# Phi fused into K's and Q's weights by six blocks of 120 rows instead of eight of 80

## Chip, cores and metric

The kernel runs on one core of a Trainium2 chip. The metric is the device time of one execution in microseconds (us), as a median over runs.

## What is computed

A token matrix x (2048 tokens of width D = 640) is normalised per row, and two branches and x itself are added. Branch A is a linear attention with 32 heads of width Dh = 20 (Hedgehog); branch B is a gated unit of width F = 1536. All tensors are bf16.

```
xn = layernorm(x)
q, k, v = split_heads(xn @ wqkv)                    # 32 heads of 20
pq, pk  = q @ w_phi[h], k @ w_phi[h]                # a 20 x 20 matrix for each head
phi_q = [softmax(pq), softmax(-pq)]; phi_k likewise # 40 features
kv = sum_s phi_k[s] * v[s];  z = sum_s phi_k[s]
A = (phi_q @ kv) / (phi_q @ z + 1e-6) @ wo
B = (silu(xn @ w1) * (xn @ w3)) @ w2
out = x + A + B
```

## The kernel before

Tokens are cut into 16 tiles of 128 (NST = 16), D into KD = 5 blocks of 128 and F into KF = 12. The order of the work is written out by hand, across all engines; every transfer is issued by SP, in program order, and each transfer takes the next of eight completion counters in turn.

1. **Start.** SP loads token tiles 0 and 1, V's weight and tiles 2 and 3. While they travel PE runs WARM = 19 products on a tile of zeros (L201), so that it is not idle. Tiles 0 to 3 are transposed by PE or DMA, normalised by DVE (L227, L269), and V of these four is made from the raw tiles (L298).
2. **Tiles 4 to 15.** They are loaded in pairs, normalised, and transposed by DMA into xnT (`by_dma`, L672). In between PE makes units of the gated branch (`glu_unit`, L442; the first, split, in L459) and V of each tile (`V`, L341 with the name pv).
3. **Fusion.** Since q @ w_phi is xn @ (wq @ w_phi), Phi goes into the weights once. `ldT` (L141) transposes columns of K's and Q's weight by DMA, NF = 8 pieces of FR = 80 rows (four heads each), into wkT and wqT. `phi_blocks` (L416, DVE) makes from w_phi and a 0/1 mask a block matrix for each piece, wphi, four heads of 20 columns wide. `fuse` (L426, PE) multiplies piece c of the transposed weight with block c, for each of the five 128-row blocks of the result, and two copies (L434, L435; ACT or DVE) bring its 640 columns from two banks to wkphi or wqphi, 320 columns each. K's fusion (`FB(0)` to `FB(4)`) stands at the end of stage 2, Q's in turns 4 to 8 of the next loop.
4. **K's loop**, 16 turns: `phi_unit` (products L341, name pk; exponentials L370; sums and reciprocals on DVE L404, L406; scaling on POOL L407), the product of phi_k and V (L483), and two units of the gated branch.
5. **Q's loop**, 20 turns: the same phi for Q (name pq), its DMA transpose, the product with kv (L518), the division, and `out_unit` (L581, L590), which sums the gated branch, wo and the residual and stores the tile.

The kernel takes exponentials without subtracting a maximum. A bound on the fused weights' norms decides whether that is safe; if it fails, the block below `tc.If(ok == 0)` (L880) computes the result anew with the maximum taken off. With this input the bound holds, and the block is jumped over. At the end (L926) SP waits for all eight completion counters, in their order, and the engines meet.

Of the kernel before, what the change touches and what calls it, by code (L numbers as in the profile page):

```python
# [8 lines left out]
P = 128  # L9
# [3 lines left out]
def kernel(  # L13
# [17 lines left out]
    nc = tc.nc  # L31
    bf = mybir.dt.bfloat16
# [5 lines left out]
    _, S, D = A_x.shape  # L38
    H, Dh = 32, 20
    F = B_w1.shape[1]  # L40
    NST, NSC, KD, KF = S // P, S // 512, D // P, F // P
    HD = D // 2
    EPS = 1e-5
    SAFE = 36.0
    BY_DMA = 4
    WARM = 19
    RAW = 4


# [2 lines left out]
    CH = 6 * 3 * Dh  # L52

    VC = 1 + 3 * Dh

    NF, FR = 8, 80

    x2 = A_x[0]
    out2 = out[0]
# [1 line left out]
    one = ctx.enter_context(tc.tile_pool(name="one", bufs=1))  # L61
# [8 lines left out]
    def pair(name):  # L70
        return psum2.tile([P, 2, 512], f32, name=name, tag="pair")
# [20 lines left out]
    wkT, wqT = [  # L92
        reg_w[:, i * NF * D : (i + 1) * NF * D].rearrange("p (c f) -> p c f", c=NF)
        for i in range(2)
    ]
# [13 lines left out]
    def slot(i):  # L109
        return phi[:, i].rearrange("p c g f -> p (c g f)")  # L110
# [3 lines left out]
    state = slot(3)[:, 0 : 2 * (NCH * VC - Dh)].bitcast(f32)  # L114
# [12 lines left out]
    def ld(dst, src):  # L127
        nc.sync.dma_start(out=dst, in_=src)  # L128
# [8 lines left out]
    wps = one.tile([P, NF, Dh], bf, name="wps")  # L137
    with tc.manual_schedule():
        def ldT(dst, i, c):
            a = i * D + c * FR  # L140
            nc.sync.dma_start_transpose(out=dst[:, c], in_=A_wqkv[:, a : a + P])  # L141


# [1 line left out]
        def ld_tiles(t, n):  # L145
            ld(
                xin[:, (t // 4) % 3, t % 4 : t % 4 + n],
                x2[t * P : (t + n) * P, :].rearrange("(t p) d -> p t d", p=P),
            )
# [7 lines left out]
        for c in range(KD):  # L157
# [9 lines left out]
        eps = one.tile([P, 1], f32, name="eps")  # L167
        nc.gpsimd.memset(eps[:], EPS)

        mask = one.tile([P, 4], bf, name="mask")  # L170
        nc.gpsimd.memset(mask[:], 1.0)
        nc.gpsimd.affine_select(
            out=mask[:], in_=mask[:], pattern=[[-20, 4]], base=0,
            channel_multiplier=1, compare_op=ALU.is_ge, fill=0.0,
        )
        nc.gpsimd.affine_select(
            out=mask[:], in_=mask[:], pattern=[[20, 4]], base=19,
            channel_multiplier=-1, compare_op=ALU.is_ge, fill=0.0,
        )

# [4 lines left out]
            out=own[:], in_=own[:], pattern=[[-64, 2], [-20, 3]], base=0,  # L185
# [3 lines left out]
            out=own[:], in_=own[:], pattern=[[64, 2], [20, 3]], base=19,  # L189
# [9 lines left out]
        def warm(n):  # L199
            for _ in range(n):  # L200
                nc.tensor.matmul(idle[:, 0:P], nought[:], nought[:])  # L201

        lit = nc.const_aps.tensor(1.0, [P, P], bf)
        for _ in range(2):
            nc.tensor.matmul(idle[:, 0:P], lit, lit)
        warm(WARM)

# [124 lines left out]
        def tile_of(t):  # L332
            return slice(t * P, (t + 1) * P)

        def by_token(cols, w, name, cut, ps=None):

            ps = ps or [bank(name), bank(name)]
            for c in range(KD):
                for i in range(2):
                    a, b = (0, cut) if i == 0 else (cut, D)  # L340
                    nc.tensor.matmul(  # L341
                        ps[i][:, 0 : b - a],
                        xnT[:, c, cols],
                        w[:, c, a:b],
                        start=(c == 0),
                        stop=(c == KD - 1),
                        skip_group_check=True,
                    )
            return ps

        def v_unit(dst, cols, ps=None):
            for piece in chunks(by_token(cols, wv, "pv", CH, ps)):
                v_copy(dst, *piece)
# [41 lines left out]
        def phi_unit(t, w, name, exps=exps, cols=None):  # L395

            ps = by_token(cols or tile_of(t), w, name, CH)
            dst = phi[:, t % 4]
            exps(ps, dst)
            rows = dst.rearrange("p c g f -> p (c g) f")[:, :, 0:60].rearrange(  # L400
                "p a (i d) -> p a i d", d=Dh
            )
            sk = work.tile([P, 2 * NCH, 3], f32, name="sk")
            nc.vector.reduce_sum(out=sk[:], in_=rows, axis=AX.X)  # L404
            rk = work.tile([P, 2 * NCH, 3], f32, name="rk")
            nc.vector.reciprocal(out=rk[:], in_=sk[:])  # L406
            nc.gpsimd.tensor_mul(  # L407
                out=rows, in0=rows, in1=rk[:, :, :, None].to_broadcast([P, 2 * NCH, 3, Dh])
            )

        wphi = one.tile([P, NF, 4, Dh], bf, name="wphi")

        def phi_blocks():
            nc.vector.tensor_mul(  # L416
                out=wphi[0:FR],
                in0=wps[0:FR, :, None, :].to_broadcast([FR, NF, 4, Dh]),
                in1=mask[0:FR, None, :, None].to_broadcast([FR, NF, 4, Dh]),
            )  # L420

        def fuse(dst, wT, d, ps, copy=None):

            for c in range(NF):
                b, i = divmod(c, 4)
                nc.tensor.matmul(  # L426
                    ps[b][:, FR * i : FR * (i + 1)],
                    wT[0:FR, c, d * P : (d + 1) * P],
                    wphi[0:FR, c],
                    start=(i == 0),  # L430
                    stop=(i == 3),
                    skip_group_check=True,
                )
            nc.scalar.copy(out=dst[:, d, 0:HD], in_=ps[0][:, 0:HD])  # L434
            (copy or nc.scalar.copy)(out=dst[:, d, HD:D], in_=ps[1][:, 0:HD])  # L435

        def glu_unit(sc, fi, banks=None):

# [40 lines left out]
        def kv_unit(t, v1, acc, first, last):  # L479

            for c in range(NCH):
                b, i = divmod(c, 6)
                nc.tensor.matmul(  # L483
                    acc[:, b, VC * i : VC * i + 1 + Dh * HC[c]],
                    phi[:, t % 4, c].rearrange("p g f -> p (g f)"),
                    v1[:, c, 0 : 1 + Dh * HC[c]],
                    start=(first and i == 0),
                    stop=last,
                    skip_group_check=True,
                )  # L490

        def kv_done(acc):

            for b, c0, n, k in ((0, 0, 6, 3), (1, 6, 4, 3), (1, 10, 1, 2)):
                a, e = VC * (c0 - 6 * b), 1 + Dh * k
                rows = acc[b][:, a : a + e * n].rearrange("p (c e) -> p c e", c=n)
                nc.vector.tensor_mul(
                    out=kvr[:, c0 : c0 + n, 0:k, 0:20],
                    in0=rows[:, :, 1:e].rearrange("p c (i d) -> p c i d", d=Dh),
                    in1=own[:, 0:1, 0:k, None].to_broadcast([P, n, k, Dh]),  # L500
                )
                nc.vector.tensor_mul(
                    out=kvr[:, c0 : c0 + n, 0:k, 20],
                    in0=rows[:, :, 0:1].to_broadcast([P, n, k]),
                    in1=own[:, 0:1, 0:k].to_broadcast([P, n, k]),
                )
# [150 lines left out]
        def unit(banks=None):  # L657
            return glu_unit(*glu.pop(0), banks)
# [12 lines left out]
        def by_dma(t):  # L671
            nc.sync.dma_start_transpose(out=xnT[:, :, tile_of(t)], in_=xin[:, (t // 4) % 3, t % 4, :])  # L672
# [78 lines left out]
        by_dma(6)  # L751
        by_dma(7)
        ld_tiles(14, 2)
        ld(wps[0:FR], A_w_phi.rearrange("h j f -> (h j) f").rearrange("(c p) f -> p c f", p=FR))
        g1()
        stats(8, 2)
        g3 = unit()
        g2()
        ldT(wkT, 1, 0)
        ldT(wkT, 1, 1)  # L760
        V(4)
        g3()
# [25 lines left out]
        V(11, two("pv"))  # L788
        ldT(wkT, 1, 4)
        ldT(wkT, 1, 5)  # L790
        ldT(wkT, 1, 6)
        g6 = unit()
        g6()
        lx(14, 2)
        by_dma(14)
        ldT(wkT, 1, 7)
        by_dma(15)
        V(12)
        g7 = unit()
# [12 lines left out]
        ps = by_token(tile_of(15), wv, "pv", CH)  # L812
# [66 lines left out]

    with tc.If(ok == 0):  # L880
        nc.gpsimd.memset(v_one[:, :, 0], 1.0)
        nc.gpsimd.memset(state, 0.0)
        halves = [state[:, 0 : 6 * VC], state[:, 6 * VC :]]
        with tc.For_i(0, NST, 1) as t:
            cols = bass.ds(t * P, P)
            v_unit(v_one, cols)
            phi_unit(0, wkphi, "pk", exps_less_max, cols)
            acc = pair("pkv")
            kv_unit(0, v_one, acc, True, True)
            for i, half in enumerate(halves):  # L890
                n = half.shape[1]
                nc.vector.tensor_tensor(out=half, in0=half, in1=acc[:, i, 0:n], op=ALU.add)
        kv_done(halves)
        with tc.For_i(0, NST, 1) as t:
            rows = bass.ds(t * P, P)
            phi_unit(0, wqphi, "pq", exps_less_max, rows)
            phi_transposed(0)
            r_unit(0, quotient_by_pool)
            o_transposed(0)
            h = hT[:, bass.ds(t, 1)].rearrange("p a f s -> p (a f) s")  # L900
            res = out_unit(h, slice(0, P), residual(rows))
            ld(out2[rows, :], res[:])
# [28 lines left out]
```

## Time and profile before

| | |
|---|---|
| time, median of 3 runs | 269.97 us (269.69 to 270.49) |
| profiled execution, time | 269.49 us |
| profiled execution, span of the trace | 267.8 us |
| granted TensorE clock, mean | 1.0 |
| busy: PE / DVE / ACT / POOL | 98% / 73% / 43% / 34% |
| DMA moved | 30.10 MB, mean 112 GB/s |

PE is TensorE's products, PEld its weight loads (which overlap the products), DVE is VectorE, ACT ScalarE, POOL GpSimd, and SPq the sequencer of SyncE, which issues transfers. L426 is line 426 of the kernel. In a chain or timeline the first number is the start in us after the span's start, the second the length in us; "idle before" tells how long the engine stood still ahead of an instruction, and what released it. Products are pipelined, so that the step from one to the next is shorter than the duration of one.

### The profile page before, as it was taken

To read this page: it belongs to the slowest core of one execution; us is meant where nothing else is said; L and a number is where in the kernel's file an instruction comes from. 1 tells how busy PE (TensorE), PEld (TensorE's weight loads), DVE (VectorE), ACT (ScalarE), POOL (GpSimd) and SP (SyncE) were. 2 spreads that over 40 slices of the span, in tenths; PEclk is the share of its full clock that TensorE was granted. 3 is DMA by queue.
4 is the path that set the end of the run, shared out by engine and by line. 5 is a ranking of instruction groups with operands and counts; after the bars stand their busy time and mean duration, and the time that the engine had idled before them with its cause. 6 is when DMAs were issued, how large, how long until landed. Compare 5 with 4: busy or idle time off the path is not lost.

```text
span 267.8 us, 5352 instructions
## 1 busy us (share of the span) xinstructions
PE 262.4 (98%) x2016; PEld 167.3 (62%) x2016; DVE 195.1 (73%) x363; ACT 114.7 (43%) x348; POOL 91.1 (34%) x88
## 2 busy tenths in 40 slices
PE   8999999999999999999999999999999999999993
PEld 7766565655555555555555555777777777777762
DVE  4789974397677777779997799967977776666431
ACT  5874454735566665445566655422222222220000
POOL 4052520064333333333544333344254333333000
PEclk9999999999999999999999999999999999999999
DMA  6999957999300000060000288856546574556631
GB/s 193 245 231 209 122 115 129 374 143 109 82 0 2 0 4 2 1 174 0 0 2 0 21 232 217 114 134 146 137 123 134 135 147 127 131 144 132 157 102 29
DMA packets 71967, 30.10 MB, mean 112 GB/s; under 512 B 58882, under 2 KB 70530, under 8 KB 71939
## 3 DMA queue, kind: packets, MB, share of 16 engines
q1 hardware_dynamic: 71938, 29.74, 50.7%
q8 instruction: 17, 0.28, 0.5%
q14 instruction: 12, 0.09, 0.2%
HBM read 13.14 MB, written 2.63 MB: 59 GB/s over the span
## 4 chain that ended last, share of the span: by engine, by line
PE 93%; DMA 3%; DVE 1%; SPq 1%; issue 0%; DVEq 0%
PE acc L581 28%; PE gp L442 19%; PE up L442 19%; PE pq L341 8%; PE pk L341 8%; PE pv L341 6%; PE pr L518 2%; PE pkv L483 2%; DMA xnT<-reg_h 1%; DMA reg_h<-in_A_x_dram 1%; SPq L128 1%; PE pf L426 1%; DVE st L227 1%; PE g L459 0%; PE gp L459 0%
## 5 line engine op out<-in xcount | busy, mean ns | idle before, releaser
L407 POOL TENSOR_TENSOR phi<-phi,rk 128x1320 bf16<-128x1320 bf16 x32 | 77.2, 2412 | 129.4 <-DVE rk L406 99.4
L442 PEld LDWEIGHTS <-w 128*128 128x128 bf16 x460 | 43.5, 98 | 47.9 <-DMA w<-in_B_w_dram 0.2
L404 DVE TENSOR_REDUCE sk<-phi 128x66 f32<-128x1320 bf16 x32 | 48.8, 1526 | 26.3 <-ACT phi L370 25.3
L442 PE MATMUL up<-xnT,w 128*128 128x512 bf16 x230 | 57.1, 379 | 0.0
L442 PE MATMUL gp<-xnT,w 128*128 128x512 bf16 x230 | 57.1, 379 | 0.0
L581 PE MATMUL acc<-reg_v,reg_h 128*128 128x320 bf16 (+2 forms) x384 | 54.9, 299 | 0.0
L341 PEld LDWEIGHTS <-xnT 128*128 128x128 bf16 x440 | 41.8, 98 | 19.1 <-DMA xnT<-reg_h 0.3
L370 ACT ACTIVATE phi<-pq 128x360 bf16<-128x360 f32 (+2 forms) x96 | 24.8, 366 | 57.7 <-issue 44.1
L581 PEld LDWEIGHTS <-reg_h 128*128 128x128 bf16 x384 | 37.3, 98 | 14.4
L453 ACT ACTIVATE th<-gp 128x512 f32<-128x512 f32 x47 | 28.4, 603 | 28.2 <-PE gp L442 28.2
L473 DVE SCALAR_TENSOR_TENSOR reg_h<-gs,up 128x512 bf16<-128x512 bf16 x47 | 32.3, 688 | 4.8
L470 DVE SCALAR_TENSOR_TENSOR gs<-th,gp 128x512 bf16<-128x512 f32 x47 | 30.9, 658 | 4.7 <-ACT th L453 4.7
L370 ACT ACTIVATE phi<-pk 128x360 bf16<-128x360 f32 (+2 forms) x96 | 24.9, 370 | 20.0 <-PE pk L341 20.0
L590 DVE TENSOR_TENSOR res<-acc,xr 128x320 bf16<-128x320 f32 (+2 forms) x32 | 14.2, 484 | 19.0 <-PE acc L581 19.0
L581 PE MATMUL acc<-reg_w,reg_v 128*128 128x320 bf16 (+2 forms) x160 | 24.5, 299 | 0.0
L341 PE MATMUL pk<-wkphi,xnT 128*128 128x360 bf16 (+1 forms) x160 | 24.4, 299 | 0.0
L341 PE MATMUL pq<-wqphi,xnT 128*128 128x360 bf16 (+1 forms) x160 | 24.3, 299 | 0.0
L406 DVE RECIPROCAL rk<-sk 128x66 f32<-128x66 f32 x32 | 18.1, 567 | 3.2
L581 PEld LDWEIGHTS <-reg_v 128*128 128x128 bf16 x160 | 15.7, 98 | 6.1
L341 PE MATMUL pv<-reg_w,xnT 128*128 128x360 bf16 x120 | 17.3, 299 | 0.0
L227 DVE BATCH_NORM_STATS2 st<-reg_h 128x6 f32<-128x320 bf16 x32 | 13.4, 476 | 4.3 <-DMA reg_h<-in_A_x_dram 4.3
L539 DVE TENSOR_TENSOR o__77<-pr,den 128x360 bf16<-128x360 f32 (+1 forms) x32 | 14.2, 485 | 0.6
(82 smaller groups left out, 161.3 us busy)
## 6 DMA issues: line engine op xcount, KB each, us to landing
w<-in_B_w_dram SPq DMA_DIRECT2D x2, 1280.0 KB, 8.2
xr<-in_A_x_dram SPq DMA_DIRECT2D x16, 160.0 KB, 2.5
out_dram<-res SPq DMA_DIRECT2D x15, 160.0 KB, 1.8
reg_h<-in_A_x_dram SPq DMA_DIRECT2D x6, 320.0 KB, 5.3
reg_v<-in_B_w_dram SPq DMA_DIRECT2D x1, 1920.0 KB, 8.5
w<-in_B_w_dram SPq DMA_DIRECT2D x4, 320.0 KB, 4.5
reg_w<-in_A_wqkv_dram SPq DMA_DIRECT2D x5, 160.0 KB, 3.3
reg_w<-in_A_wo_dram SPq DMA_DIRECT2D x1, 800.0 KB, 8.1
```

The lines of the kernel that those rows point to most:

```text
L227: nc.vector.bn_stats(out=st[:, i, :], in_=xt[:, i * HD : (i + 1) * HD])
L341: nc.tensor.matmul(ps[i][:, 0 : b - a], xnT[:, c, cols], w[:, c, a:b], start=(c == 0), stop=(c == KD - 1), skip_group_check=True,)
L370: nc.scalar.activation(out=dst[:, c0 : c0 + n, g, 0:k], in_=p.rearrange("p (c f) -> p c f", c=n), func=AF.Exp, scale=1.0 - 2.0 * g,)
L404: nc.vector.reduce_sum(out=sk[:], in_=rows, axis=AX.X)
L406: nc.vector.reciprocal(out=rk[:], in_=sk[:])
L407: nc.gpsimd.tensor_mul(out=rows, in0=rows, in1=rk[:, :, :, None].to_broadcast([P, 2 * NCH, 3, Dh]))
L442: nc.tensor.matmul(ps, w[:, c, fi * P : (fi + 1) * P], xnT[:, c, sc * 512 : (sc + 1) * 512], start=(c == 0), stop=(c == KD - 1),)
L453: nc.scalar.activation(out=th[:], in_=gp, func=AF.Tanh, scale=0.5)
L470: nc.vector.scalar_tensor_tensor(out=gs[:], in0=th[:], scalar=1.0, in1=gp, op0=ALU.add, op1=ALU.mult)
L473: nc.vector.scalar_tensor_tensor(out=hT[:, 4 * sc : 4 * sc + 4, fi, :], in0=gs[:].rearrange("p (t s) -> p t s", t=4), scalar=0.5, in1=up.r ...
L539: nc.vector.tensor_mul(out=o_[:, t % 2, Dh * h0 : Dh * h1].rearrange("p (h d) -> p h d", d=Dh), in0=p3[:, :, 0:20], in1=den[:, h0:h1, None ...
L581: nc.tensor.matmul(ps[:, 0 : b - a], rows[j][0], rows[j][1][:, a:b], start=(j == 0), stop=(j == len(rows) - 1),)
```

## The change

The weights' columns are cut into NF = 6 pieces of FR = 120 rows, six heads each. Since 640 is not a multiple of 120, the sixth piece starts at row 520 and overlaps the fifth; of its block only the last two heads (40 columns) are used. The first bank then holds three pieces (360 columns = CH), the second two pieces and the short one (280), and the copies are cut there. w_phi is loaded in two transfers: five pieces, then the overlapping one. Two `ldT` of K's weight are dropped, and two of Q's by the shorter loop. WARM becomes 20. In the block of the failed bound one memset of 651 columns becomes seven of 93.

```diff
-    WARM = 19
+    WARM = 20
...
-    NF, FR = 8, 80
+    NF, FR, LH = 6, 120, 6
+    AT = [120 * c for c in range(5)] + [D - 120]
...
-            a = i * D + c * FR
+            a = i * D + AT[c]
...
-        mask = one.tile([P, 4], bf, name="mask")
+        mask = one.tile([P, LH], bf, name="mask")
...
-        wphi = one.tile([P, NF, 4, Dh], bf, name="wphi")
+        wphi = one.tile([P, NF, LH, Dh], bf, name="wphi")
...
-                b, i = divmod(c, 4)
+                b, i = divmod(c, 3)
+                h0 = 4 if c == NF - 1 else 0
                 nc.tensor.matmul(
-                    ps[b][:, FR * i : FR * (i + 1)],
+                    ps[b][:, FR * i : FR * i + Dh * (LH - h0)],
                     wT[0:FR, c, d * P : (d + 1) * P],
-                    wphi[0:FR, c],
+                    wphi[0:FR, c, h0:LH],
                     start=(i == 0),
-                    stop=(i == 3),
+                    stop=(i == 2),
                     skip_group_check=True,
                 )
-            nc.scalar.copy(out=dst[:, d, 0:HD], in_=ps[0][:, 0:HD])
-            (copy or nc.scalar.copy)(out=dst[:, d, HD:D], in_=ps[1][:, 0:HD])
+            nc.scalar.copy(out=dst[:, d, 0:CH], in_=ps[0][:, 0:CH])
+            (copy or nc.scalar.copy)(out=dst[:, d, CH:D], in_=ps[1][:, 0 : D - CH])
...
-        ld(wps[0:FR], A_w_phi.rearrange("h j f -> (h j) f").rearrange("(c p) f -> p c f", p=FR))
+        w_phi = A_w_phi.rearrange("h j f -> (h j) f")
+        ld(wps[0:FR, 0:5], w_phi[0 : 5 * FR].rearrange("(c p) f -> p c f", p=FR))
+        ld(wps[0:FR, 5], w_phi[D - FR : D])
...
         ldT(wkT, 1, 4)
         ldT(wkT, 1, 5)
-        ldT(wkT, 1, 6)
         g6 = unit()
         g6()
         lx(14, 2)
         by_dma(14)
-        ldT(wkT, 1, 7)
         by_dma(15)
...
-        nc.gpsimd.memset(state, 0.0)
+        for i in range(7):
+            nc.gpsimd.memset(state[:, 93 * i : 93 * (i + 1)], 0.0)
```

More of the change, by code (lines that the diff above doesn't have):

```diff
@@ L168 @@
         nc.gpsimd.memset(eps[:], EPS)
-        mask = one.tile([P, 4], bf, name="mask")
+        mask = one.tile([P, LH], bf, name="mask")
         nc.gpsimd.memset(mask[:], 1.0)
         nc.gpsimd.affine_select(
-            out=mask[:], in_=mask[:], pattern=[[-20, 4]], base=0,
+            out=mask[:], in_=mask[:], pattern=[[-20, LH]], base=0,
             channel_multiplier=1, compare_op=ALU.is_ge, fill=0.0,
@@ L176 @@
         nc.gpsimd.affine_select(
-            out=mask[:], in_=mask[:], pattern=[[20, 4]], base=19,
+            out=mask[:], in_=mask[:], pattern=[[20, LH]], base=19,
             channel_multiplier=-1, compare_op=ALU.is_ge, fill=0.0,
@@ L417, in phi_blocks @@
                 out=wphi[0:FR],
-                in0=wps[0:FR, :, None, :].to_broadcast([FR, NF, 4, Dh]),
-                in1=mask[0:FR, None, :, None].to_broadcast([FR, NF, 4, Dh]),
+                in0=wps[0:FR, :, None, :].to_broadcast([FR, NF, LH, Dh]),
+                in1=mask[0:FR, None, :, None].to_broadcast([FR, NF, LH, Dh]),
             )
```

## Prediction

> **What bounds the kernel now.** I read the table of engines first, then the slices, the busy time by stage, the chain in order of time, and last the queue of SP, which issues every transfer.
>
> ```profile
> PE 262.4 (98%) x2016; PEld 167.3 (62%) x2016; DVE 195.1 (73%) x363; ACT 114.7 (43%) x348; POOL 91.1 (34%) x88
> ...
> DMA  6999957999300000060000288856546574556631
> ```
> ```profile
> 10.00:14.50 4.50, 4.30 (x39) 3.43 (x38) 3.40 (x11) 3.77 (x11) 0.95 (x3) 1.00 0.96 167
> 14.50:23.00 8.50, 8.42 (x55) 5.30 (x55) 7.81 (x20) 4.71 (x10) 3.16 (x13) 1.00 1.11 263
> 23.00:31.00 8.00, 8.00 (x50) 4.56 (x48) 7.38 (x21) 4.04 (x14) 3.94 (x13) 1.00 1.01 137
> 31.00:45.00 14.00, 14.00 (x88) 8.49 (x87) 9.10 (x19) 6.54 (x21) 2.53 (x11) 1.00 0.68 128
> 45.00:50.00 5.00, 5.00 (x66) 3.88 (x65) 3.06 (x6) 2.59 (x9) 0.00 (x0) 1.00 0.84 264
> 50.00:145.00 95.00, 95.00 (x668) 52.20 (x666) 74.60 (x101) 54.02 (x160) 37.41 (x16) 1.00 0.27 51
> 145.00:263.50 118.50, 118.48 (x979) 82.14 (x976) 83.98 (x170) 32.63 (x112) 39.78 (x17) 1.00 0.58 133
> ```
> ```profile
> 4.09 3.71 DMA reg_h<-in_A_x_dram
> 7.82 0.90 DVE st L227 x2
> ...
> 10.55 3.98 DMA xnT<-reg_h
> ...
> 14.58 1.25 PE g L459 x10
> ...
> 30.99 5.43 PE pv L341 x40
> ...
> 263.51 0.42 DVE res L590
> ```
>
> In the rows by stage a stretch and its length are followed by the busy time of PE, PE's weight loads, DVE, ACT and POOL, the granted clock (1.00 throughout), the DMA share and GB/s. PE is busy 98% of the span, and by stage it is stricter than that: from 23.00 to 263.50 it is busy in all but 0.02 us. Busy is not the same as saturated, but the chain agrees: from 14.58 to the last tile every step starts where the one before it ended. What stands outside that stretch is a head of 14.58 us (token tile 2 is loaded, normalised, transposed by DMA) and a tail from 263.51 to 267.8. The DMA engines are full (1.11 and 1.01) exactly while the token tiles and Phi's pieces are being transposed. So an edit can pay in three ways only: fewer PE cycles, a shorter head, a shorter tail. It can cost by making PE wait, most easily between 14.5 and 36, where transfers are tight.
>
> **The fused weights on PE.** Each of the ten fusions goes from eight products of 80 columns to five of 120 and one of 40; both are 640 columns.
>
> ```profile
> 45.62 0.57 PE pf L426 x16
> ...
> 49.77 1.36 PE pk L341 x10
> ...
> 60.33 0.32 PE pkv L483 x11
> ```
>
> Sixteen products of 80 columns took 0.57 us: 36 ns each, 0.285 us a fusion. Ten products of K's unit (five of 360 columns, five of 280, 3200 in all) took 1.36 us, 0.425 ns a column; by that row a fusion costs 640 x 0.425 = 0.272 us. The other end: at the old rate of 36/80 = 0.45 ns a column a piece of 120 costs 54 ns, and the short one no less than the step of the products of 61 and 41 columns, 0.32/11 = 29 ns; 5 x 54 + 29 = 0.299 us. Ten fusions lie between -0.13 and +0.14 us. I take 0, the middle, because the old pieces already ran near their column count. The Trainium skill (TensorE: Matmul & The Clock Gate, "Back-to-back issue gap") states columns over 2.4 plus 2.5 ns, with a floor of about 25 ns; by that it is 287.5 ns against 286.7, an estimate of +0.01 us over ten. That agrees with the 36 ns of the row.
>
> **Copies and the masked product.**
>
> ```profile
> L434 ACT CAST wkphi<-pf x5: 425/432/472, 45.9 to 49.8; 128x320 bf16<-128x320 f32 x5
> ```
> ```profile
> L416 DVE TENSOR_TENSOR wphi<-wps,mask x1: 811/811/811, 34.2 to 34.2; 80x640 bf16<-80x640 bf16 x1
> ...
> DMA to landing us min/median/max: 3.6/3.6/3.6
> ```
>
> The copies keep their number and total width (360 + 280 for 320 + 320), so ACT's first one grows by at most 432 x 40/320 = 54 ns and the second shrinks by the same. The masked product grows from 640 to 720 columns: 811 x 720/640 = 912 ns, 0.1 us more of DVE at 34.2 while PE runs without a gap; nothing waits for it before 45.6. The blocks of w_phi landed 3.6 us after 22.73, 8 us before they are used, so their two pieces may be late. All this is at nothing; if DVE's cover were gone it would be 0.1 us.
>
> **SP's queue.** Two transposes of K's weight are removed and two of Q's, and the load of w_phi becomes two.
>
> ```profile
> 22.73 0.46 SPq L128 DMA_DIRECT2D wps<-in_A_w_phi_dram  x1
> 23.24 2.50 SPq L141 DMA_TRANSPOSE reg_w<-in_A_wqkv_dram  x2
> 25.84 2.74 SPq L672 DMA_TRANSPOSE xnT<-reg_h  x2
> 28.64 1.94 SPq L141 DMA_TRANSPOSE reg_w<-in_A_wqkv_dram  x1
> 30.66 1.23 SPq L672 DMA_TRANSPOSE xnT<-reg_h  x1
> ```
> ```profile
> 30.77 5.32 PEld L341 LDWEIGHTS <-xnT 128*128 128x128 bf16 x40 [0.27 <-DMA xnT<-reg_h]
> ```
> ```profile
> L672 SPq DMA_TRANSPOSE xnT<-reg_h x13: 1205/1227/1415, 10.6 to 43.8; - x13
> ...
> DMA to landing us min/median/max: 2.4/3.0/4.9
> ```
>
> SP issues without a pause here, so the second load (0.46 us and a gap of 0.05) pushes the two wkT transposes and tiles 8 to 11 back by 0.51 us. Tile 8 is the tight one: the weight load at 30.77 had already waited 0.27 us for it, and its product begins at 30.99, so 0.22 us is free. If nothing absorbs the shift, PE waits 0.29 us. Two rows say that much is absorbed: tile 8 took the longest of all landings (25.84 to 30.77 is the 4.9), so it stood behind earlier packets and not behind its issue; and SP itself was held, 1.94 us for one transpose where 1.23 is usual. I take +0.05, ends 0 and +0.29. The removed transposes come later in the queue: two times 1.2 us off before tiles 14 and 15, where PE does not wait, so no gain; Q's are off the path, being needed only in the fifth turn of K's loop.
>
> **The warm-up product.**
>
> ```profile
> 1.05 1.95 PEld L201 LDWEIGHTS <-nought 128*128 128x128 bf16 x19
> ...
> 3.07 0.46 PEld L287 LDWEIGHTS <-reg_h 128*128 128x128 bf16 x5
> ```
>
> Nineteen took 1.95 us, so one more is 0.10 us, and the first transposes follow at once. It can delay PE's transposes of tiles 0 and 1 by that. The chain of the head does not pass through them: it goes from the load of tiles 2 and 3 (4.09) over DVE to the DMA transpose of tile 2. I take 0, with +0.10 as the other end.
>
> **The tail.** The seven memsets stand on a path that this input does not take.
>
> ```profile
> 254.72 0.34 SPq L128 DMA_DIRECT2D out_dram<-res  x1
> ...
> 259.68 4.62 SPq L128 DMA_DIRECT2D out_dram<-res  x3
> ```
> ```profile
> out_dram<-res SPq DMA_DIRECT2D x1, 64.0 KB, 2.2
> ```
> ```profile
> L926 SPq EVENT_SEMAPHORE  x10: 17/28/28, 265.2 to 267.7; - x10
> ...
> L926 SPq DRAIN  x3: 7/7/13, 266.5 to 266.8; - x3
> ```
>
> The last store's issue ends at 264.30; with an issue of 0.34 us, as for the store before, it began at 263.96 and landed 2.2 us later, at 266.15. SP then drains at 266.5. Between lie SP's closing waits, which go through the eight completion counters in a fixed order. Transfers take these counters in turn: in the program before, the last store has the third, so five waits still follow its landing, some 0.35 us or 0.07 each. The change has three transfers fewer, and in the changed program's order the last store has the eighth. Nothing is left to wait for behind it: five times 0.07 less, up to -0.35, and 0 if the spacing is not what I infer. I take -0.25.
>
> **The sum.** 0 + 0 + 0.05 + 0 - 0.25 = -0.2 us on the profiled execution: 269.49 (span 267.8 and 1.69 around it) becomes 269.3. The median, 269.97, stands 0.48 above that execution, and gives 269.8.
>
> **Rivals.**
> *Tile 10 late (slower).* Tile 10 is issued at 30.66, and with the shift at 31.17; its product is due at 30.99 + 2 x 1.36 = 33.71. At the least landing, 2.4, it comes at 33.57, in time; at 4.1, between the median and the worst, at 35.27, and PE stands still for 1.56 us: 269.97 - 0.25 + 1.56 = 271.3. It decides once the landing takes over 3.6 us, which leaves 0.81 net. For: DMA is full there, and two tiles just before took over four. Against: that jam was over by then, SP having been held up in it.
> *The head opens (faster).* Tile 2's transpose took 3.98 us against a median of 3.0. PE fetches its own code by DMA, and one more instruction pair moves that fetch; if it leaves the transpose alone, PE begins up to 1.0 us earlier. But what is late next caps it:
>
> ```profile
> 17.68 3.07 PEld L442 LDWEIGHTS <-w 128*128 128x128 bf16 x15 [0.17 <-DMA w<-in_B_w_dram]
> ```
> That weight is used at 18.00, so some 0.32 us is free unless its load moves too. With the best ends, -0.32 - 0.13 - 0.35 = -0.80: 269.2, at the edge of what counts as faster.
> *The jump (no gain).* Six more instructions shift where POOL's closing code lies.
>
> ```profile
> L880 PEldq COMPARE_BRANCH  x1: 940/940/940, 261.3 to 261.3; - x1
> ...
> L880 SPq COMPARE_BRANCH  x1: 53/53/53, 264.3 to 264.3; - x1
> ```
> PE's jump over the failed-bound body took 0.94 us, hidden behind its queue; SP's took 0.05. If a fetch of that size fell into POOL's closing code, which is on the path, the time is 269.8 + 0.9 = 270.7, still within 0.3%. The Trainium skill (Runtime: NRT & Kernel Launch, "Instruction fetch mechanics") states that a taken branch to a page that is not held must fetch it first; PE's 940 ns against SP's 53 agrees, though only the first shows such a stall.
>
> **How the numbers follow.** About 0.3%, 0.81 us, is what a measurement of this kernel can tell from no change. The forecast has 0.61 and the jump 0.04: no change, 0.65. Tile 10 has 0.20, the open head 0.15. The forecast's own ends are -0.8 (-0.13 - 0.35 - 0.32) and +0.5 (0.14 + 0.29 + 0.10) around 269.97, widened below by the spread of the runs, 0.28 (269.97 - 269.69): 268.9 to 270.5. The range reaches halfway to the slower rival, 271.0, which leaves out some 0.15 there and little below.
>
> **What would show it.** Right: twenty fewer products on the pf line (60 for 80) at the same total; 14.58 and 30.99 in the chain moved by under 0.3; SP's last drain closer to the last landing by about 0.3. Wrong: a wait of PE for xnT in the stretch from 30 to 36, or a first product of g (L459, line numbers one to three higher) a microsecond from 14.58.

## The result and the profile after

The changed kernel takes 268.66 us (median of 6 runs, 268.41 to 268.92) against 270.13 for the kernel before in the same comparison: a ratio of 0.9946, with a 95% interval of 0.9933 to 0.9959. It is 1.47 us faster, and 0.24 us below the range that was forecast. Its profiled execution took 268.62 us, with a span of 266.8.

The page after, engines and slices (the rows that answer to the first fence of the prediction):

```profile
PE 262.0 (98%) x1979; PEld 167.7 (63%) x1997; DVE 195.0 (73%) x363; ACT 114.8 (43%) x348; POOL 91.1 (34%) x88
...
DMA  6998856976000000060000098455655555556931
```

PE is still busy for 98% of the span, now with fewer instructions (this trace lacks the records of some products; the weight loads, 1997 for 2016, show the 19 pairs that went). The gain is not visible here, nor in the stages around the fusion (columns as in the prediction):

```profile
23.00:31.00 8.00, 7.95 (x48) 4.63 (x48) 7.37 (x21) 4.17 (x14) 3.69 (x14) 1.00 0.89 135
31.00:45.00 14.00, 13.95 (x87) 8.39 (x87) 9.77 (x21) 6.25 (x21) 3.10 (x11) 1.00 0.61 119
```

The chain in order of time shows where it isn't:

```profile
14.87 1.09 PE g L461 x10
...
31.12 5.58 PE pv L342 x40
...
45.89 0.57 PE pf L428 x12
...
50.05 1.36 PE pk L342 x10
...
263.79 0.42 DVE res L592
```

Every one of these steps starts later than its counterpart before (the last addition at 263.79 against 263.51), although the whole span is 1.0 us shorter. So all of the gain lies behind the last addition: from its start to the end of the span it was 267.78 - 263.51 = 4.27 us and is 266.79 - 263.79 = 3.00, which is 1.27 less, while 0.28 was lost ahead of it. The transfers of the last two stores and the engines' closing drains show two places of it. First the changed kernel:

```profile
out_dram<-res SPq DMA_DIRECT2D x1, 96.0 KB, 2.4
out_dram<-res SPq DMA_DIRECT2D x1, 64.0 KB, 1.5
```
```profile
L929 POOLq DRAIN  x3: 34/50/82, 246.0 to 266.5; - x3
L929 SPq DRAIN  x3: 7/7/13, 266.0 to 266.3; - x3
...
L929 POOLq EVENT_SEMAPHORE_RANGE_CLEAR  x1: 135/135/135, 266.4 to 266.4; - x1
```

Then those rows of the kernel before that the prediction did not read (the 64 KB store, 2.2 us, it did):

```profile
out_dram<-res SPq DMA_DIRECT2D x1, 96.0 KB, 3.6
```
```profile
L926 POOLq DRAIN  x3: 34/50/215, 245.8 to 267.5; - x3
...
L926 POOLq EVENT_SEMAPHORE_RANGE_CLEAR  x1: 135/135/135, 267.4 to 267.4; - x1
```

The stores land in 2.4 and 1.5 us for 3.6 and 2.2, and POOL's longest drain, the one just before it clears the semaphores, takes 82 ns for 215; it also begins 0.09 us behind POOL's last wait in place of 0.40. Counted from the start of the last addition, the records of the two traces give three steps:

| step | before | after | difference |
|---|---|---|---|
| last landing | 2.62 | 1.97 | -0.65 |
| from there to SP's first drain | 0.38 | 0.21 | -0.17 |
| from there to the end | 1.27 | 0.82 | -0.45 |

### The profile page after: what moved, and what is told of

Read it like the earlier page. It is cut to its first block, busy times and chain, and to the rows that moved or that the text cites. A ratio compares the mean times of both kernels' runs of the same rounds, so it can differ in the third digit from the quotient of the medians.

```text
span 266.8 us, 5294 instructions
## 1 busy us (share of the span) xinstructions
PE 262.0 (98%) x1979; PEld 167.7 (63%) x1997; DVE 195.0 (73%) x363; ACT 114.8 (43%) x348; POOL 91.1 (34%) x88
## 4 chain that ended last, share of the span: by engine, by line
PE 98%; issue 0%; DVE 0%
PE acc L583 28%; PE up L444 19%; PE gp L444 18%; PE pq L342 8%; PE pk L342 8%; PE pv L342 6%; PE pr L520 2%; PE pkv L485 2%; PE pv L299 2%; PE pf L428 1%; PE idle L202 1%; PE pst L288 1%; PE g L461 1%; PE v L299 1%; PE gp L461 0%; PE up L461 0%
## 5 line engine op out<-in xcount | busy, mean ns | idle before, releaser
L444 PE MATMUL gp<-xnT,w 128*128 128x512 bf16 x215 | 55.8, 378 | 0.7
```

The source lines that it names most:

```text
L444: nc.tensor.matmul(ps, w[:, c, fi * P : (fi + 1) * P], xnT[:, c, sc * 512 : (sc + 1) * 512], start=(c == 0), stop=(c == KD - 1),)
```

## Experiments

The question for the runs was which part of the edit made each of the three steps, and whether the fusion had any share. Three theories stood against each other: POOL's closing code lies elsewhere once seven memsets stand in front of it; the last store takes another completion counter, since fewer transfers are issued; and PE's count of instructions moves the fetch of PE's own code, which travels through the same DMA engines as the stores. The rival to all three was that the fused weights themselves, or the head, had become faster.

**Seven memsets alone, in the kernel before**

```diff
-        nc.gpsimd.memset(state, 0.0)
+        for i in range(7):
+            nc.gpsimd.memset(state[:, 93 * i : 93 * (i + 1)], 0.0)
```

> The kernel before with the seven memsets alone. Theory P (POOL's closing code is fetched right after its jump instead of at the very end): POOL's drain at the end loses its 0.4 us gap, 0.44 us faster than before, ratio 0.9984, and a POOL code fetch near 244 us appears. Rival F (the gain is made by the fusion's six pieces and the four transposes that went): no change, ratio 1.000, same gap.

Measured: 269.28 us against 269.59, ratio 0.9986 (0.9976 to 0.9996). Its closing drains:

```profile
L927 POOLq DRAIN  x3: 34/50/82, 246.0 to 266.9; - x3
L927 SPq DRAIN  x3: 7/7/13, 266.4 to 266.7; - x3
```

POOL's drain is at 82 ns, and from SP's first drain to the end it is 0.82 us, just as in the changed kernel. Six more instructions that never run are worth 0.45 us at the end of the trace, and they do it alone; the medians are 0.31 us apart.

**The changed kernel with one memset**

```diff
-        for i in range(7):
-            nc.gpsimd.memset(state[:, 93 * i : 93 * (i + 1)], 0.0)
+        nc.gpsimd.memset(state, 0.0)
```

> The kernel after with the one memset of before. Theory P: POOL's gap at the end is back, 0.44 us slower than after, ratio to before 0.9962. Rival F: as after, 0.9946.

Measured: 269.12 us, ratio 0.9983 (0.9972 to 0.9993).

```profile
L928 POOLq DRAIN  x3: 34/50/215, 246.2 to 267.1; - x3
L928 SPq DRAIN  x3: 7/7/13, 266.1 to 266.4; - x3
```

The 215 ns are back, and the last step is 1.26 us; the other two steps stay as in the changed kernel (landing at 1.97, drain 0.21 behind it). The memsets thus act on the last step and on no other. Nothing in their place is computed: the block is jumped over in all these kernels.

**The kernel before with forty more instructions on PE**

Two units of the gated branch are computed in halves of 256 columns, as its first unit is already. Each of them is then 20 products of half the length in place of 10, so that PE executes 20 more products and 20 more weight loads, as against the 20 and 20 fewer that the ten fusions in the change need.

```diff
+    HALVES = ((0, 4), (0, 5))
...
+            if (sc, fi) in HALVES:
+                for ps, w in ((gp, w1), (up, w3)):
+                    for i in range(2):
+                        glu_half(i, w, sc, fi, ps)
+                return glu_done(sc, fi, gp, up)
```

> The kernel before with two units of the gated branch in halves, 40 more instructions on PE and nothing else. Theory C: PE's last code fetch moves off the stores, up to 0.6 us faster than before less 0.05 us for the halves, ratio 0.998. Rival F: 0.05 us slower, 1.000.

Measured: 269.51 us, ratio 0.9998 (0.9987 to 1.001): no difference in time. The profiled execution shows one all the same:

```profile
out_dram<-res SPq DMA_DIRECT2D x1, 96.0 KB, 2.6
out_dram<-res SPq DMA_DIRECT2D x1, 64.0 KB, 1.5
```

The stores land as in the changed kernel, 1.98 us after the last addition's start, with the memset, the counters and the fusion of before. What moved can be seen among the DMA queues. In the kernel before, in a stretch of 1.7 us that starts 0.1 us after its last addition (263.51):

```profile
q1 hardware_dynamic: 146, 0.07, 15.3%
q8 instruction: 1, 0.02, 3.5%
```

One packet of 16 KB on a queue of instructions took 3.5% of 16 engines' 1.7 us, which is 0.95 us on one engine, beside the stores on q1. In the kernel with forty more instructions the same packet is found in a stretch that starts 0.8 us ahead of the last addition (263.53), together with the 96 KB store:

```profile
q1 hardware_dynamic: 144, 0.10, 19.5%
q8 instruction: 1, 0.02, 3.5%
```

It is gone before the last store is issued. In the trace before, 15 of the 16 DMA engines' parts of that store had landed by 1.98 us after the addition's start, and the sixteenth came at 2.62. The other three profiles with a late landing (in the table further down) look the same: one part alone is late, at 2.24 to 2.62. That the packets on this queue are PE's code is read from their spacing: in the trace before, PE runs some 253 products and weight loads from one 16 KB packet to the next, and no other engine has more than 488 instructions in the whole span.

**The changed kernel with as many products as before**

The same two units in halves, and 19 warm-up products.

```diff
-    WARM = 20
+    WARM = 19
...
+    HALVES = ((0, 4), (0, 5))
```

> The kernel after with WARM 19 and two units of the gated branch in halves of 256 columns, so that PE executes as many instructions as in before; the fusion stays at six pieces. Theory C (PE's code fetch after its jump falls among the packets of the last stores in before, and no longer in after): the fetch is back at about 0.2 us after PE's last product, the last store lands 2.1 us after its issue instead of 1.5, 0.6 us slower than after, ratio to before 0.997. Rival F: 0.9946, as the fusion is unchanged.

Measured: 268.79 us, ratio 0.9969 (0.9957 to 0.9981). The fetch moved later by 0.7 us, to between -0.25 and 0.75 us about the start of the last addition, but not back to where it is before (0.20 to 1.16), so it did not meet the last store: that landed at 2.00, and the tail stayed at 3.00. This run therefore did not undo the third part, as it was built to. Count alone does not fix the place of the fetch to a few tenths. So it is shown that forty more instructions move the fetch off the last store in the kernel before, its fusion untouched; that the forty fewer did it in the changed kernel is not shown.

**A different counter for the last store, in the kernel before**

Five loads of 16 bytes in K's loop, long before the end, turn the last store's counter from the third to the eighth.

```diff
+    spare = one.tile([1, 40], bf, name="spare")
...
+            if i == 13:
+                for k in range(5):
+                    ld(spare[0:1, 8 * k : 8 * k + 8], x2[0:1, 8 * k : 8 * k + 8])
```

> The kernel before with five loads of 16 bytes added in the 13th turn of K's loop, where SP is idle, so that the last store takes the eighth completion counter in place of the third. Theory T: SP drains 0.18 us earlier after the last addition, about 2.8 us if PE's code fetch still meets the stores, ratio 0.9993; POOL's gap stays. Rival: the order of the counters costs nothing, 1.000.

Measured: 269.34 us, ratio 0.9981 (0.9969 to 0.9994). SP's waits from 263.0 to the end, by line and releaser, with the sum, the count and the longest:

```profile
SPq L930 <- DMA out_dram<-res: 0.5, 1, 0.5
SPq L884 <- SPq L884: 0.2, 1, 0.2
```

SP now reaches the eighth counter before the last store has landed, waits once, and drains 0.08 us behind the landing in place of 0.38. The order of counters does what the prediction took it to do, and a little more. Its second row explains the more: SP's jump over the failed block held it for 0.2 us here and for 0.5 in the kernel before, counted to SP's next instruction. (The 53 ns that the prediction read are the jump's own row, and are the same in both.) POOL's pause of 0.40 us is there too, but one instruction earlier; its longest drain took 132 ns, and the last step 1.18 us. In the changed kernel the jump holds it for 0.5 too, and SP waits for no store at all, since no such row is left there:

```profile
SPq L929 <- PEq L929: 0.6, 2, 0.5
SPq L882 <- SPq L882: 0.5, 1, 0.5
```

There the end is set by SP's own walk through the eight counters, some 0.06 us each, which begins late because of the jump: it drains at 2.18 with the landing at 1.97.

**All three in the kernel before, its eight pieces kept; and the changed kernel again**

The first has the seven memsets, the five loads and the two units in halves; the second is the changed kernel without any edit, on the same chip.

```diff
+    HALVES = ((0, 4), (0, 5))
...
+            if i == 13:
+                for k in range(5):
+                    ld(spare[0:1, 8 * k : 8 * k + 8], x2[0:1, 8 * k : 8 * k + 8])
...
-        nc.gpsimd.memset(state, 0.0)
+        for i in range(7):
+            nc.gpsimd.memset(state[:, 93 * i : 93 * (i + 1)], 0.0)
```

> The kernel before with the fusion in eight pieces, and the three things of the end alone: seven memsets, five tiny loads, two gated units in halves (40 more instructions on PE). Theory T: as much as the whole change, tail 3.0 us, 0.87 to 1.25 less 0.05, ratio 0.9956 to 0.997. Rival F: only POOL's part, 0.9984.

> The kernel after once more, on the chip of this call, to be set against the kernels beside it. Theory T (all of the gain lies behind the last product: POOL's closing code 0.44 us, counter order 0.18, PE's code fetch off the stores 0.25 to 0.63): 0.87 to 1.25 us under before, ratio 0.9954 to 0.9968; the stretch from the start of the last DVE addition to the end 3.0 us again. Rival F (the fusion brings the rest): 0.9946.

Measured: 268.70 us, ratio 0.9966 (0.9949 to 0.9982), for the kernel before with the three by-products; 268.78, ratio 0.9965 (0.9951 to 0.9979), for the change. They cannot be told apart. Closing rows of the first:

```profile
L937 POOLq DRAIN  x3: 34/50/82, 246.2 to 266.5; - x3
L937 SPq DRAIN  x3: 7/7/13, 266.0 to 266.3; - x3
```
```profile
SPq L937 <- DMA out_dram<-res: 0.2, 1, 0.2
SPq L890 <- SPq L890: 0.2, 1, 0.2
```

Its tail is 2.87 us. All that the change gains is had without fusing by six pieces.

**The fusion by six pieces alone**

One memset, 19 warm-up products, and three loads of 16 bytes, so that the last store is on the third counter again.

```diff
-    WARM = 20
+    WARM = 19
...
+            if i == 13:
+                for k in range(3):
+                    ld(spare[0:1, 8 * k : 8 * k + 8], x2[0:1, 8 * k : 8 * k + 8])
...
-        for i in range(7):
-            nc.gpsimd.memset(state[:, 93 * i : 93 * (i + 1)], 0.0)
+        nc.gpsimd.memset(state, 0.0)
```

> The fusion in six pieces with the end as in before where that can be had: one memset, WARM 19, three tiny loads in K's loop so that the last store has the third counter again. PE still executes 40 instructions fewer. Theory T: POOL's gap and the five waits are back, tail 3.6 us against 4.3 of before, ratio 0.9977 to 1.000. Rival F: 0.9946 to 0.997.

Measured: 269.26 us, ratio 0.9986 (0.9972 to 1.000).

```profile
L932 POOLq DRAIN  x3: 34/50/216, 245.9 to 267.0; - x3
L932 SPq DRAIN  x3: 7/7/13, 266.0 to 266.3; - x3
```

POOL's 0.45 us and the 0.39 us behind the landing are back. Only the early landing (1.98) is left; PE still has its forty fewer instructions.

**An equal kernel, and a version made from the findings**

The kernel before was run against itself. Beside it ran the changed kernel with the transposes of K's weight for pieces 1 to 3 moved behind those of token tiles 9, 11 and 13, and the same with eight loads of 16 bytes, which keep the last store on the eighth counter.

```diff
-        ldT(wkT, 1, 1)
...
+        ldT(wkT, 1, 1)
```

> The kernel before itself, for a second profile and for what the comparison shows of two equal kernels: ratio 1.000 within 0.0013. Theory T: PE's last code fetch again at 0 to 0.2 us behind the start of the last addition, tail 3.9 to 4.3 us, POOL's gap of 0.4 us.

> The kernel after with K's transposes 1, 2 and 3 issued behind the token tiles 8 and 9, 10 and 11, 12 and 13 in place of ahead of them. If PE's waits for tiles 8 to 11 (0 to 0.75 us, another amount in each profile) come from standing behind those transposes, the stretch from the first V product of tile 4 to the first product of the fusion is 24.4 us with no wait, 0 to 0.3 us better than after, ratio 0.996. Rival: the waits come from code fetches that stop any transpose, and stay, 0.9965.

> a_order with eight loads of 16 bytes in K's loop: the last store keeps the eighth counter, but SP's code stands elsewhere, and its jump at the end should cost 0.14 us instead of 0.47 as in the kernel with five such loads; tail 2.87 us instead of 3.0. Expected 0.13 us under a_order, ratio 0.9955. Rival: the loads' place does not matter, 0.996.

Measured: the kernel before against itself 269.46 us, ratio 0.9985 (0.9972 to 0.9998). A kernel can thus appear 0.15% (0.4 us) from itself, its interval just missing 1; no difference of that size between the runs above counts by its time alone. Its profiled tail is 4.26 us, as the first time, with 3.7 and 2.2 us for the last two stores. The moved transposes gave 268.48, ratio 0.9950 (0.9931 to 0.9969), and with the eight loads 268.41, ratio 0.9945 (0.9924 to 0.9966). PE has no wait at token tiles 8 to 11 in the first one's profile, all forty weight loads following each other:

```profile
30.63 5.47 PEld L342 LDWEIGHTS <-xnT 128*128 128x128 bf16 x40
```

That does not show that the move did it: from the first product of V of tile 4 to the first of the fusion it is 24.38 us here, and 24.38 as well in the second profile of the changed kernel, whose transposes were not moved. In the kernel with eight loads SP's jump is at 0.2 us and the tail at 2.87. Both times are at or below the changed kernel's 268.66, from another comparison, and by time neither can be told from it.

All profiles side by side, in us after the start of the last addition (the fetch is PE's 16 KB packet nearest the end of its work; in the six kernels with fewer PE instructions than before, one more follows, but it begins at 1.95 or later, when the last store is landing):

| kernel | counter | memsets | fetch ends | last landing | to SP's drain | to the end | tail |
|---|---|---|---|---|---|---|---|
| before | 3rd | 1 | 1.16 | 2.62 | 0.38 | 1.27 | 4.27 |
| before, again | 3rd | 1 | 1.32 | 2.62 | 0.38 | 1.26 | 4.26 |
| + seven memsets | 3rd | 7 | 0.99 | 2.24 | 0.38 | 0.82 | 3.44 |
| + five loads | 8th | 1 | 1.23 | 2.26 | 0.08 | 1.18 | 3.52 |
| + halves | 3rd | 1 | 0.23 | 1.98 | 0.39 | 1.25 | 3.62 |
| + all three | 8th | 7 | 0.21 | 1.97 | 0.09 | 0.81 | 2.87 |
| fusion alone | 3rd | 1 | -0.26 | 1.98 | 0.39 | 1.26 | 3.63 |
| changed, one memset | 8th | 1 | 0.18 | 1.97 | 0.21 | 1.26 | 3.44 |
| changed, count as before | 8th | 7 | 0.75 | 2.00 | 0.19 | 0.81 | 3.00 |
| changed | 8th | 7 | -0.01 | 1.97 | 0.21 | 0.82 | 3.00 |
| changed, again | 8th | 7 | 0.17 | 1.97 | 0.22 | 0.81 | 3.00 |
| changed, transposes moved | 8th | 7 | -0.26 | 1.98 | 0.21 | 0.81 | 3.00 |
| the same + eight loads | 8th | 7 | -0.19 | 1.98 | 0.08 | 0.81 | 2.87 |

The last store is issued at 0.45 in all of them. Wherever the fetch ended by 0.75, it landed within 0.03 us of 1.98; wherever it ended at 0.99 or later, it landed 0.26 to 0.64 us later than that.

## Why the prediction was wrong, step by step

**The tail is the step that failed.** The term "The tail" was put at -0.25 us with ends of -0.35 and 0; it measured -1.27. Its mechanism was right, but it is one of three. Behind the landing 0.17 us was saved for the 0.25 taken: a counter costs 0.06 us for the 0.07 inferred, and SP's late jump kept back another 0.13 that the kernel with all three by-products did save. The other two it missed, each with a row in sight:
- The 2.2 us of the 64 KB store were read as how long such a store takes. The row of the fifteen larger stores on the page, 160 KB in 1.8 us, says that 2.2 for 64 KB is late. Something held it, and that can go away: 0.65 us.
- POOL's closing code was considered only as something that could become worse.

**The rival of the jump had its sign wrong.** It had six more instructions bring a stall into POOL's closing code. The stall was already there, as the 215 ns drain before shows beside the 82 ns after, and with six more it went: -0.45 in place of +0.9. The Trainium skill (Runtime: NRT & Kernel Launch, "Instruction fetch mechanics") has a taken branch to a page that is not held wait for its fetch. By that rule the stall depends on where the code lies and so can go either way; both signs should have been priced. The traces do not show that such a fetch is the cause here. In both kernels POOL takes its jump 20.29 us ahead of the last addition and goes on 2.47 us later; the 215 ns come only at the end. With seven memsets an 8 KB packet of code does appear some 19 us before the last addition, as was expected, and with one memset it comes at the very end instead; but there it begins behind the drain (in the trace before 4.31 us after the addition's start, with the drain at 3.59), so it cannot be what held it. That the memsets remove the 0.45 us is shown in both directions; by what mechanism stays open.

**The fusion at 0: right.** One fusion step of the changed kernel:

```profile
L428 PE MATMUL pf<-wphi,reg_w x60: 182/215/218, 45.7 to 100.4; 120*128 120x120 bf16 x50, 120*128 120x40 bf16 x10
...
L436 ACT CAST wkphi<-pf x5: 458/465/505, 46.2 to 50.1; 128x360 bf16<-128x360 f32 x5
```

Sixty products for eighty, and twelve of them took the same 0.57 us as sixteen did. From the first one to the first pk it was 4.16 us and is 4.16, from there to the first pq 94.73 and 94.72. ACT's first copy grew by 33 ns at the median (54 at most was said), and the masked product measured 902 ns for the 912 worked out; both remained hidden.

**SP's queue: right within its ends.** The queue and the weight loads after:

```profile
22.73 1.00 SPq L129 DMA_DIRECT2D wps<-in_A_w_phi_dram  x2
23.78 2.49 SPq L142 DMA_TRANSPOSE reg_w<-in_A_wqkv_dram  x2
26.38 3.52 SPq L674 DMA_TRANSPOSE xnT<-reg_h  x2
```
```profile
30.86 2.64 PEld L342 LDWEIGHTS <-xnT 128*128 128x128 bf16 x20 [0.24 <-DMA xnT<-reg_h]
33.81 2.56 PEld L342 LDWEIGHTS <-xnT 128*128 128x128 bf16 x20 [0.31 <-DMA xnT<-reg_h]
```

The transposes moved back by 0.54 us (0.51 was worked out), and tile 10 was late, as the slower rival had it, but by far less: its load waited 0.31 us where the rival had 1.56, and the four tiles took 5.58 us for 5.43. The sign of being wrong that the prediction named, a wait for xnT between 30 and 36, is thus there. But it is no mark of the change, since the kernel before has the same wait in its second profile:

```profile
33.46 2.56 PEld L341 LDWEIGHTS <-xnT 128*128 128x128 bf16 x20 [0.32 <-DMA xnT<-reg_h]
```

From the first product of V of tile 4 to that of the fusion it was 24.38 us before, 24.53 in the kernel before again, 24.52 and 24.38 in the two runs of the change; over all thirteen profiles it is 24.38 to 25.12 with eight pieces and 24.38 to 24.84 with six. That 0.15 comes and goes in both kernels, so the change doesn't own it, and that the term came out within its ends is chance.

**The warm-up and the head: right in the main.** The first transposes begin at 3.16 us in place of 3.08. The open head did not occur: 14.87 in the chain for 14.58, and PE's first product of V of tile 4 at 21.21 for 21.08, 0.03 past the end of 0.10. That 0.13 is no effect of the change that the runs can show: over the thirteen profiles the same product begins at 20.85 to 21.62 with eight pieces and at 20.75 to 21.66 with six. The head thus varies from one execution to the next by up to 0.9 us, nearly as much as the whole gain.

**The sum.** 0.13 (head) + 0.15 (tiles 8 to 11) - 1.27 (tail) = -0.99 on the span. The first two terms vary as much among profiles of one kernel; only the third belongs to the change. The two comparisons of the change have their medians 1.47 and 0.90 us apart, on either side of it. The range was too narrow below, as it held no case in which anything but the counters shortened the tail.

**What stays open.** Of the gain, 0.45 (POOL) and 0.17 (counters) are the same to 0.02 us in every profile of their kind but one (1.18 for 1.26, with the five loads alone). How often the fetch meets the last store in executions without a profile is not known: both profiles of before show it, but the kernel with forty more PE instructions, which doesn't, has no better time (0.65 us would be a ratio of 0.9976; its interval begins at 0.9987). Where the boundaries of POOL's and SP's code lie was not tried either.

## What to carry to other kernels

When PE runs without a gap, as here, an edit that keeps its columns and adds no wait has little to move there, so the difference must be looked for ahead of its first product and behind its last: read the kernel's end row by row, each store's landing against its like, each engine's last drain. An edit that alters how many instructions or transfers there are can also move code fetches, closing code and completion counters, and a stall that the profile of before already has at such a place is a gain in waiting, to be priced with both signs. To know what did it, put the by-products of the change into the old kernel without the change, and run an unchanged kernel against itself beside it.

## What the runs showed of the hardware that was not expected

- PE's code comes in packets of 16 KB through the same DMA engines as data, about 1 us each (0.92 to 1.53 in the table's runs), and a store whose share on that engine stands behind one lands up to 0.64 us late.
- Seven memsets that never execute shorten the kernel's end by 0.45 us: POOL's drain 82 ns for 215, and the closing semaphore work begins sooner.
- The same jump held SP for 0.5 us or for 0.2, depending on the kernel: 0.2 in the kernels with five or eight more loads, 0.5 in all others. It showed only where the last store is on the last counter; on the third, SP still waits for a store after its jump, by 0.2 to 0.9 us.
- PE's jump took from 0.37 us to 3.80. The 3.62 of the changed kernel cost nothing: PE went on 1.48 us after the last addition's start, and SP drains at 2.18.
